# A fused state-space scan and ELU feed-forward block on one Trainium2 core: three changes of order in the opening, a weight load ahead of a B load, a negative part ahead of a weight piece's magnitude, and a clamp and shift ahead of two masks

## The chip, the core and the metric

The kernel runs on one core of a Trainium2 chip. The core has a matrix engine (TensorE, PE in the profile, with its weight loads as PEld), a vector engine (VectorE, DVE), an activation engine (ScalarE, ACT), a general engine (GpSimd, POOL), a queue engine that here only issues transfers (SyncE, SP), and 16 DMA engines. Each engine takes its own instructions strictly in the order in which they were written. Engines wait for one another by semaphores. The metric is the time of one execution on the device in microseconds. Lower is better.

## The reference

The first half is a chunked state-space scan ("mamba2_ssd") over 4 batches, 8 heads and 768 tokens, with 32 channels per head and a state of 16. The second half is a feed-forward block with an ELU between its two matrix products, on 3072 tokens of width 256 and a hidden width of 2048.

```python
cum = np.cumsum(la, axis=-1)                         # la = log of clipped a, per chunk
L = np.exp(cum[:, :, :, None] - cum[:, :, None, :])  # times the causal mask
M = np.einsum('bhin,bhjn->bhij', Cc, Bc) * L
y = np.einsum('bhij,bhjd->bhid', M, xc) + np.einsum('bhin,bhnd->bhid', Cc, state) * np.exp(cum)[..., None]
state = decay_full * state + np.sum(Bx, axis=2)      # Bx = B x, each step decayed to the chunk's end
...
h = x @ w_in                                         # x is y with heads and channels side by side
g = np.where(h > 0.0, h, np.exp(np.minimum(h, 0.0)) - 1.0)
return (g @ w_out).astype(np.float32)
```

The two weight matrices are handed over as 64-bit floats. [...]

## The kernel before

The tokens are worked in twelve blocks of 256, numbered 0 to 11: block 0 and block 1 are the first 256 tokens of two batches, 2 and 3 the next 256 of the same two, and so on. For each block the scan makes a 256 x 256 slab `yT`, and the feed-forward part multiplies it by pieces of `w_in` (`l1`), applies the ELU (`elu`), and multiplies by pieces of `w_out` (`l2`). The order of all instructions is written out by hand: there is no scheduler that moves them, and the statements at the end of the kernel function are that order.

There are 16 weight pieces, 0 to 7 of `w_in` and 8 to 15 of `w_out`, each 512 KB as 64-bit words. A piece is turned into 32-bit floats by these steps, and the names come back in all that follows:

- `w_load` (line 184) issues the transfer on SP.
- `w_abs` (205, ACT) takes the magnitude of the high words. For pieces 1 and 2 it writes to PSUM, the matrix engine's accumulator memory; for the others to SBUF, the main on-chip memory.
- `w_low` (214, ACT) brings the low words into a small float.
- `w_sign` (229, DVE) takes the sign bit, SBUF to SBUF.
- `w_high_a` (237, DVE) clamps the magnitude. It runs in PSUM for piece 2 and from SBUF to SBUF for piece 3.
- `w_high_b` (244, DVE) shifts the magnitude and joins the sign. `w_high` is `w_high_a` and then `w_high_b`.
- `w_sum` (254, POOL) adds the low part. After it the piece can be used by `l1`.

The ELU of one product is three instructions. `begin_elu` (731, ACT) takes the negative part with a Relu of the negated product. `elu` then issues the Exp (738, ACT) and the join (739, DVE). `elu` calls `begin_elu` itself unless it has been called already.

Block 1's part of the scan in the opening needs: B and C in the "square" and the token layout. `load_bc(1)` loads B for the two halves of the tokens as two transfers of 64-byte rows (140); `load_squares(1, 1)` loads C (124). `turn_square(1, 1)` (468, DVE) transposes C in 32 x 32 blocks. `turn_b(1)` transposes B on PE (432) and copies it on ACT (435). `mask_heads(1)` multiplies the turned C by two head masks, two DVE instructions (478), which write `ctm`. `turn_exp(1)` (459, DVE) multiplies the turned C by the decay `ec`; both its inputs lie in SBUF. `scores(1)` (583, PE) needs `ctm` and the turned B. `weigh` (592, DVE) multiplies the scores by the decays `L`. `sums(1)` (613, PE) and `states(1)` (628 and 630 on DVE, 635 on POOL) make the running states. `across(1)` (661, PE) and `inside(1)` (679, PE) make block 1's result, which ACT and DVE copy to `yT` (696, 694). On POOL, `scaled(1)` (423) multiplies B by a decay, and `rest_of_sums` (343) prepares decays for the later blocks; it stands right behind `w_sum(3)`.

After that the long middle begins with `l1(1, 0)`, the first product on block 1's result.

The part of the written order that the change touches reads, before:

```python
w_abs(2); w_low(2, nc.scalar); w_high_a(2); w_sign(2); w_high_b(2); w_sum(2)
elu()
turn_square(1, 1)
first_decays(1, 0, 1, 2, 3); l1(0, 1); w_abs(3)
w_low(3, nc.scalar); w_sign(3)
mask_heads(1)
w_high(3)
turn_b(1)
```

Of the kernel before, what the change touches and what calls it, by code (L numbers as in the profile page):

```python
# [33 lines left out]
def kernel(  # L34
# [56 lines left out]
    def psum(shape, name):  # L91
        return p_a.tile(shape, F32, tag="a", name=name)
# [18 lines left out]
    def place(n):  # L111

        return 2 * (n // (2 * NG)) + n % 2, n // 2 % NG
# [5 lines left out]
    def load_squares(n, k):  # L119
        b, g = place(n)  # L120
        squares = st[n]["bc"].rearrange("p k u h n -> p k (u h n)").rearrange(
            "p k (m r) -> p k m r", m=2)
        for m in range(2):
            nc.sync.dma_start(
                out=squares[:, k, m],
                in_=(B, C)[k][b, m:NH:2, g * BLK:(g + 1) * BLK, :].rearrange(
                    "q (c t) n -> q c (t n)", t=8))

    def load_bc(n, c_queue=nc.sync, us=(0, 1)):
        b, g = place(n)  # L130
        if "bc" not in st.setdefault(n, {}):
            st[n]["bc"] = raw.tile([P, 2, 2, NH, N], F32, tag="bc", name="bc", bufs=2)
        if n > 3:
            for k in range(2):
                load_squares(n, k)
            return
        for u in us:
            sl = slice((2 * g + u) * P, (2 * g + u + 1) * P)
            for k, src in enumerate((B,) if n == 1 else (B, C)):
                (nc.sync, c_queue)[k].dma_start(  # L140
                    out=st[n]["bc"][:, k, u], in_=src[b, :, sl, :].rearrange("h s n -> s h n"))
# [50 lines left out]
    def w_words(i):  # L192
        words = w_raw[i].rearrange("p k (f t) -> p k f t", t=2)
        return words[:, :, :, 0], words[:, :, :, 1]

    def w_parts_of(i):
        if i not in w_mag:
            both = big([P, 2, 2, CW], U32, "mag")
            w_mag[i], w_sgn[i] = both[:, 0], both[:, 1]

    def w_abs(i, cols=slice(None)):
        if i in (1, 2) or cols.start:
            w_abs_of[i, cols.start] = psum([P, 2, CW], "ps_mag").bitcast(U32)
        w_parts_of(i)
        nc.scalar.activation(
            w_abs_of.get((i, cols.start), w_mag[i])[:, :, cols].bitcast(F32),
            w_words(i)[1][:, :, cols].bitcast(F32), ACT.Abs)
# [4 lines left out]
    def w_low(i, eng, cols=slice(None)):  # L212
        if eng is nc.scalar:
            eng.activation(  # L214
                pieces[i][0][:, :, cols], w_words(i)[0][:, :, cols], ACT.Identity,
                scale=2.0 ** -51, bias=two)
        else:
            eng.tensor_scalar(
                out=pieces[i][0], in0=w_words(i)[0], scalar1=2.0 ** -51, scalar2=2.0,
                op0=ALU.mult, op1=ALU.add)  # L220

    def w_sign(i, cols=slice(None), eng=nc.vector):
        w_parts_of(i)
        if eng is nc.gpsimd:
            eng.tensor_scalar(
                out=w_sgn[i][:, :, cols], in0=w_words(i)[1][:, :, cols].bitcast(mybir.dt.int32),
                scalar1=0.0, scalar2=2.0 ** 31, op0=ALU.is_lt, op1=ALU.mult)
            return
        nc.vector.tensor_scalar(
            out=w_sgn[i][:, :, cols], in0=w_words(i)[1][:, :, cols], scalar1=0x80000000,  # L230
            scalar2=None, op0=ALU.bitwise_and)

    def w_high_a(i, cols=slice(None)):
        mag = w_abs_of.get((i, cols.start), w_mag[i])[:, :, cols]


        nc.vector.tensor_scalar(
            out=mag.bitcast(F32), in0=mag.bitcast(F32),
            scalar1=high_word_as_f32(0x38000000), scalar2=high_word_as_f32(0x47EFFFFF),
            op0=ALU.max, op1=ALU.min)  # L240

    def w_high_b(i, cols=slice(None), ks=slice(None)):
        mag, sgn = w_mag[i][:, ks, cols], w_sgn[i][:, ks, cols]
        nc.vector.scalar_tensor_tensor(
            out=mag, in0=w_abs_of.get((i, cols.start), w_mag[i])[:, ks, cols], scalar=3, in1=sgn,
            op0=ALU.logical_shift_left, op1=ALU.bitwise_xor)

    def w_high(i):
        w_high_a(i)
        w_high_b(i)  # L250

    def w_sum(i, cols=slice(None), ks=slice(None)):
        w = pieces[i][0].bitcast(U32)[:, ks, cols]
        nc.gpsimd.tensor_tensor(out=w, in0=w_mag[i][:, ks, cols], in1=w, op=ALU.add)  # L254
# [172 lines left out]
    def turn_b(n):  # L427

        s = st[n]
        tb = psum([P, 2, P], "ps_tb")  # L430
        for u in range(2):
            nc.tensor.transpose(
                out=tb[:, u], in_=s["bc"][:, 0, u].rearrange("p h n -> p (h n)"),
                identity=ident)
        nc.scalar.copy(out=s["bt"], in_=tb)
# [25 lines left out]
    def turn_square(n, k):  # L461


        s = st[n]
        if "squares" not in s:
            s["squares"] = att.tile([P, 2, 2, P], F32, tag="bct", name="bct", bufs=2)
            s["bt"], s["ct"] = s["squares"][:, 0], s["squares"][:, 1]
        nc.vector.transpose(
            out=s["squares"][:, k].rearrange("p u i -> p (u i)").rearrange("p (c t) -> p t c", t=8),
            in_=s["bc"].rearrange("p k u h n -> p k (u h n)").rearrange(  # L470
                "p k (m t n) -> p k t m n", m=2, n=N)[:, k])

    def mask_heads(n, eng=nc.vector):
        s = st[n]
        s["ctm"] = att.tile([P, 2, 2, P], F32, tag="ctm", name="ctm")
        if eng is nc.vector:
            for k in range(2):
                eng.tensor_scalar(
                    out=s["ctm"][:, :, k], in0=s["ct"], scalar1=hmask2[:, k:k + 1],
                    scalar2=None, op0=ALU.mult)  # L480
            return
        eng.tensor_tensor(
            out=s["ctm"], in0=s["ct"].unsqueeze(2).to_broadcast([P, 2, 2, P]),
            in1=hmask2.unsqueeze(1).unsqueeze(3).to_broadcast([P, 2, 2, P]), op=ALU.mult)
# [22 lines left out]
    def first_cum(n):  # L507

        for k in range(2):
            for v in range(2):  # L510
                for q in range(4):
                    rows, row = slice(32 * q, 32 * q + 32), 32 * q + NH * n + 2 * q + k
                    nc.tensor.matmul(
                        out=st[n]["low"][q][Q * v:Q * v + Q, k],
                        lhsT=ident[rows, row:row + 1].to_broadcast([32, Q]),
                        rhs=F0[rows, :, Q * v:Q * v + Q], start=False, stop=False,
                        tile_position=(32 * q, Q * v), skip_group_check=True)
        for u in range(2):
            for q in range(4):
                rows, r0 = slice(32 * q, 32 * q + 32), 32 * q + NH * n + 2 * q  # L520
                nc.tensor.matmul(
                    out=st[n]["low"][q][:, :, u], lhsT=F0[rows, u],
                    rhs=minus[rows, r0:r0 + 2].unsqueeze(2).to_broadcast([32, 2, Q]),
                    start=False, stop=True, tile_position=(32 * q, 0), skip_group_check=True)
# [179 lines left out]
    def g_tile(n, i):  # L704

        if (n // 2, i) not in g_of:
            g_of[n // 2, i] = big([P, 2, 2, BLK], F32, "g")
        return g_of[n // 2, i]
# [19 lines left out]
    def begin_elu():  # L728

        begun.append(ffn.tile([P, 2, BLK], F32, tag="e", name="e", bufs=2))  # L730
        nc.scalar.activation(begun[0], lag[0][2], ACT.Relu, scale=-1.0)

    def elu():
        if not begun:
            begin_elu()
        n, i, ps = lag.pop(0)
        e = begun.pop()
        nc.scalar.activation(e, e, ACT.Exp, scale=-1.0)
        nc.vector.scalar_tensor_tensor(
            out=g_tile(n, i)[:, :, n % 2], in0=e, scalar=1.0, in1=ps,  # L740
            op0=ALU.subtract, op1=ALU.max)
# [303 lines left out]
    w_load(1)  # L1045
    load_bc(1, us=())
    load_squares(1, 1)
    load_bc(1, us=(0,))
    w_load(2)
    load_bc(1, us=(1,))  # L1050
    w_load(3)
    load_x(1, 4)
    half = [slice(0, P), slice(P, 2 * P)]
# [47 lines left out]
    spread_cum(2)  # L1101
    first_low(1, p_o)
    first_cum(1)
    w_abs(2)
    w_low(2, nc.scalar)
    w_high_a(2)
    w_sign(2)
    w_high_b(2)
    w_sum(2)
    elu()  # L1110
    turn_square(1, 1)
    first_decays(1, 0, 1, 2, 3)
    l1(0, 1)
    w_abs(3)
    w_low(3, nc.scalar)
    w_sign(3)
    mask_heads(1)
    w_high(3)
    turn_b(1)
    nc.scalar.activation(F[:, 1], F[:, 0], ACT.Exp)  # L1120
    write_flat_exp()
    load_bc(2)
# [356 lines left out]
```

## Time and profile before

| what | value |
| --- | --- |
| median of 3 runs | 341.44 us (341.13 to 341.68) |
| the profiled execution's own time | 342.17 us |
| its span from first to last instruction | 340.5 us, 9647 instructions |
| PE busy | 333.4 us, 98% of the span |
| DVE, ACT, POOL busy | 286.5, 259.2, 214.9 us |
| granted TensorE clock | 1.00 throughout |

PE is busy nearly all the time. Cut into stretches of the span, PE is busy for 308.70 us of the 312.15 us from 28.35 us to the end, and for 24.7 us of the 28.35 us before that. So an order that makes PE wait longer or shorter in the opening moves the whole of the rest, and the opening is the place to read.

In the profile's groups a line of this kernel can stand for many uses. Line 254 is the last step of every weight piece, and line 739 the join of every early ELU. The reader has to go by time within the opening to tell them apart. Start times below are from the span's start.

### The profile page before, as it was taken

To read this page: it belongs to the slowest core of one execution; us is meant where nothing else is said; L and a number is where in the kernel's file an instruction comes from. 1 tells how busy PE (TensorE), PEld (TensorE's weight loads), DVE (VectorE), ACT (ScalarE), POOL (GpSimd) and SP (SyncE) were. 2 spreads that over 40 slices of the span, in tenths; PEclk is the share of its full clock that TensorE was granted. 3 is DMA by queue.
4 is the path that set the end of the run, shared out by engine and by line. 5 is a ranking of instruction groups with operands and counts; after the bars stand their busy time and mean duration, and the time that the engine had idled before them with its cause. 6 is when DMAs were issued, how large, how long until landed. Compare 5 with 4: busy or idle time off the path is not lost.

```text
span 340.5 us, 9647 instructions
## 1 busy us (share of the span) xinstructions
PE 333.4 (98%) x3742; PEld 289.8 (85%) x3742; DVE 286.5 (84%) x509; ACT 259.2 (76%) x537; POOL 214.9 (63%) x242
## 2 busy tenths in 40 slices
PE   8889999999999999999999999999999999999996
PEld 6568878888888888888899888899888899999995
DVE  3798988889897889898989998989995977997951
ACT  4598989699858599857898866898866789897501
POOL 5644545456979396988578978478984346685000
PEclk9999999999999999999999999999999999999999
DMA  8899999372578378570869591769441754230101
GB/s 136 207 249 169 315 184 267 80 148 73 190 145 316 119 184 301 176 204 14 277 184 184 179 276 26 272 181 172 135 166 29 253 166 142 93 128 0 34 0 62
DMA packets 82955, 54.79 MB, mean 161 GB/s; under 512 B 59038, under 2 KB 68574, under 8 KB 82910
## 3 DMA queue, kind: packets, MB, share of 16 engines
q1 hardware_dynamic: 80734, 53.98, 56.7%
q8 instruction: 29, 0.48, 0.6%
q10 hardware_dynamic: 2176, 0.20, 0.5%
q14 instruction: 16, 0.13, 0.1%
HBM read 44.53 MB, written 9.63 MB: 159 GB/s over the span
## 4 chain that ended last, share of the span: by engine, by line
PE 91%; SPq 3%; ACT 2%; DMA 2%; DVE 1%; issue 0%; POOL 0%; DVEq 0%; ACTq 0%
PE ps_o L982 24%; PE ps_h L833 20%; PE ps_o L886 12%; PE ps_h L718 10%; PE ps_w L833 10%; PE ps_both L982 6%; PE ps_y L679 3%; PE ps_y L661 2%; DMA w<-in_moe_w_in_dram 2%; PE ps_g L583 2%; PE ps_st L613 1%; PE ps_high L982 1%; SPq L184 1%; SPq L140 0%; SPq L156 0%; ACT w_in L214 0%
## 5 line engine op out<-in xcount | busy, mean ns | idle before, releaser
L900 POOL TENSOR_TENSOR g_words<-g_words,g_low 128x512 fp32r<-128x512 f32 x62 | 82.5, 1333 | 51.1 <-DVE g_low L924 28.4
L982 PE MATMUL ps_o<-o_words,g_words 128*128 128x256 f32 x448 | 83.7, 284 | 0.0
L982 PEld LDWEIGHTS ps_o<-o_words,g_words 128*128 128x128 f32 x448 | 72.7, 191 | 6.1 <-POOL g_words L900 1.1
L861 ACT ACTIVATE e<-ps_h 128x512 f32<-128x512 f32 x72 | 43.1, 598 | 36.3 <-DVE ps_h L849 36.3
L868 DVE SCALAR_TENSOR_TENSOR g<-e,ps_h 128x512 f32<-128x512 f32 x72 | 49.2, 684 | 19.3 <-ACT e L862 17.0
L924 DVE SCALAR_TENSOR_TENSOR g_low<-g_words,g 128x512 fp32r<-128x512 f32 x72 | 63.8, 891 | 0.0
L982 PE MATMUL ps_o<-o_low,g_low 128*128 128x256 f32 x224 | 63.3, 283 | 0.0
L849 DVE SCALAR_TENSOR_TENSOR ps_h<-ps_h,e 128x512 f32<-128x512 f32 x72 | 49.7, 691 | 2.7 <-ACT e L841 2.6
L833 PE MATMUL ps_w<-y_both,w_words 128*128 128x512 f32 x144 | 48.7, 419 | 0.0
L718 PE MATMUL ps_h<-yT,w_in 128*128 128x256 f32 (+1 forms) x208 | 45.2, 367 | 2.4 <-POOL w_in L254 2.4
L841 ACT ACTIVATE e<-ps_w 128x512 f32<-128x512 f32 x72 | 42.0, 583 | 7.3 <-PE ps_w L833 7.3
L862 ACT ACTIVATE e<-e 128x512 f32<-128x512 f32 x72 | 45.5, 632 | 2.3
L886 PE MATMUL ps_o<-w_out,g 128*128 128x256 f32 x192 | 45.5, 380 | 0.0
L833 PE MATMUL ps_h<-y,w_words 128*128 128x512 f32 x144 | 45.4, 396 | 0.1
L833 PE MATMUL ps_h<-y,w 128*128 128x512 f32 x144 | 44.6, 391 | 0.0
L923 ACT ACTIVATE g_words<-g 128x512 fp32r<-128x512 f32 x72 | 43.6, 625 | 0.0
L718 PEld LDWEIGHTS ps_h<-yT,w_in 128*128 128x128 f32 x208 | 36.3, 190 | 8.4 <-POOL w_in L254 3.5
L982 PEld LDWEIGHTS ps_o<-o_low,g_low 128*128 128x128 f32 x224 | 42.7, 191 | 0.0
L886 PEld LDWEIGHTS ps_o<-w_out,g 128*128 128x128 f32 x192 | 36.1, 189 | 5.4
L833 PEld LDWEIGHTS ps_h<-y,w_words 128*128 128x128 f32 x144 | 26.6, 188 | 7.0 <-PE ps_w L833 0.9
L833 PEld LDWEIGHTS ps_h<-y,w 128*128 128x128 f32 x144 | 27.0, 188 | 6.2
L833 PEld LDWEIGHTS ps_w<-y_both,w_words 128*128 128x128 f32 x144 | 23.6, 191 | 1.9 <-DVE y_both L817 0.2
(133 smaller groups left out, 552.3 us busy)
## 6 DMA issues: line engine op xcount, KB each, us to landing
w_words<-w_kept SPq DMA_DIRECT2D x28, 512.0 KB
w<-w_kept SPq DMA_DIRECT2D x28, 256.0 KB
L<-flat SPq DMA_DIRECT2D x20, 256.0 KB
w<-in_moe_w_out_dram SPq DMA_DIRECT2D x8, 512.0 KB
w_kept<-w_words SPq DMA_DIRECT2D x8, 512.0 KB
w<-in_moe_w_in_dram SPq DMA_DIRECT2D x7, 512.0 KB
xr<-in_x_dram SPq DMA_DIRECT2D x24, 128.0 KB
out_dram<-eo SPq DMA_DIRECT2D x18, 128.0 KB
```

The source lines that it names most:

```text
L718: nc.tensor.matmul(out=ps[:, j, toks], lhsT=w_in[i][:, k, j * P:(j + 1) * P], rhs=yT[n // 2][:, k, n % 2].rearrange("p u i -> p (u i)")[:, ...
L833: nc.tensor.matmul(out=ps, lhsT=lhs[:, k], rhs=rhs[:, k], start=k == 0 and lhs is not w0, stop=k == KC - 1 and lhs is not w1)
L841: nc.scalar.activation(e, both, ACT.Copy, scale=WORD)
L849: nc.vector.scalar_tensor_tensor(out=high, in0=high, scalar=WORD - 1.0, in1=e, op0=ALU.mult, op1=ALU.add)
L861: nc.scalar.activation(e, high, ACT.Relu, scale=-1.0)
L862: nc.scalar.activation(e, e, ACT.Exp, scale=-1.0)
L868: nc.vector.scalar_tensor_tensor(out=g_tile(n, m // 2)[:, m % 2].rearrange("p b i -> p (b i)"), in0=e, scalar=1.0, in1=h, op0=ALU.subtract ...
L886: nc.tensor.matmul(out=o_of[n][:, ts], lhsT=g_of[n // 2, j][:, m % 2, n % 2, ts * P:(ts + 1) * P], rhs=w_out[j][:, m % 2], start=(m == 0 a ...
L900: nc.gpsimd.tensor_tensor(out=out, in0=in0, in1=in1, op=ALU.subtract)
L923: yield nc.scalar.activation(words[:, 0], g, ACT.Copy, scale=NEAR / WORD)
L924: yield nc.vector.scalar_tensor_tensor(out=low, in0=words[:, 0].bitcast(F32), scalar=WORD, in1=g, op0=ALU.mult, op1=ALU.subtract)
L982: nc.tensor.matmul(out=ps, lhsT=lhs, rhs=rhs, start=lhs is both_g and first > 0 or lhs is g1 and first > 1, stop=last and lhs is not g1, s ...
```

## The change

Three things are put in another order. No instruction is added or removed.

1. On SP, the load of weight piece 2 goes ahead of the first half of block 1's B. The two halves of B then follow one another.
2. `begin_elu` for the first product goes ahead of piece 2's magnitude on ACT, so that only its Exp is left behind piece 2's low words. On DVE, the transposition of C goes ahead of the first ELU's join.
3. On DVE, piece 3's clamp and shift (`w_high(3)`) go ahead of the two masks of C. On ACT, the copy of the turned B goes ahead of piece 3's low words.

```diff
     w_load(1)
     load_bc(1, us=())
     load_squares(1, 1)
-    load_bc(1, us=(0,))
     w_load(2)
-    load_bc(1, us=(1,))
+    load_bc(1)
     w_load(3)
     load_x(1, 4)
...
     spread_cum(2)
     first_low(1, p_o)
     first_cum(1)
+    begin_elu()
     w_abs(2)
     w_low(2, nc.scalar)
     w_high_a(2)
     w_sign(2)
     w_high_b(2)
     w_sum(2)
+    turn_square(1, 1)
     elu()
-    turn_square(1, 1)
     first_decays(1, 0, 1, 2, 3)
     l1(0, 1)
     w_abs(3)
+    turn_b(1)
     w_low(3, nc.scalar)
     w_sign(3)
+    w_high(3)
     mask_heads(1)
-    w_high(3)
-    turn_b(1)
     nc.scalar.activation(F[:, 1], F[:, 0], ACT.Exp)
```

The order on PE and on POOL is the same before and after.

## The prediction

> **What bounds the kernel now.** I read the page's busy shares and its chain first, then the chain in order of time for the opening, then the order of DVE and POOL there, and last the places where a DVE and a POOL instruction meet.
>
> ```profile
> PE 333.4 (98%) x3742; PEld 289.8 (85%) x3742; DVE 286.5 (84%) x509; ACT 259.2 (76%) x537; POOL 214.9 (63%) x242
> ...
> PE 91%; SPq 3%; ACT 2%; DMA 2%; DVE 1%; issue 0%; POOL 0%; DVEq 0%; ACTq 0%
> ```
>
> ```profile
> 28.35:340.50 312.15, 308.70 (x3232) 272.22 (x3232) 266.71 (x458) 240.70 (x493) 200.17 (x206) 1.00 0.55 158
> ```
>
> From 28.35 us on PE works without a stop that matters (busy 308.70 of 312.15 us in the stretch of the second fence). The kernel's time moves with the start of the first product on block 1, at 28.35. This is the chain that leads there:
>
> ```profile
> 9.98 6.41 DMA w<-in_moe_w_in_dram
> ...
> 16.47 0.63 ACT ps_mag L205
> ...
> 19.89 0.69 ACT mag L205
> ...
> 23.27 0.69 DVE g L739
> ...
> 25.21 0.14 DVE S_new L628
> ...
> 28.35 1.67 PE ps_h L718 x11
> ```
>
> Weight piece 2 lands at 16.39; its magnitude starts at 16.47 on ACT, after 2.11 us of idling. ACT then carries the chain until the second ELU's join on DVE at 23.27. From there DVE runs back to back to the states at 25.13, and PE follows. What the join's 23.27 becomes is what 28.35 becomes. Now the two engines that the third edit touches:
>
> ```profile
> 20.05 0.54 DVE L229 TENSOR_SCALAR mag<-w 128x512 uint32<-128x512 uint32 x1
> 20.51 0.97 DVE L478 TENSOR_SCALAR ctm<-bct,hmask 128x256 f32<-128x256 f32 x2
> 21.40 0.42 DVE L237 TENSOR_SCALAR mag<-mag 128x512 f32<-128x512 f32 x1
> 21.85 0.69 DVE L244 SCALAR_TENSOR_TENSOR mag<-mag 128x512 uint32<-128x512 uint32 x1
> 22.46 0.42 DVE L459 TENSOR_TENSOR bct<-bct,ec 128x256 f32<-128x256 f32 x1
> ```
>
> ```profile
> 19.02 1.28 POOL L254 TENSOR_TENSOR w_in<-mag,w_in 128x512 uint32<-128x512 uint32 x1 [2.45 <-ACT e L738]
> 20.26 0.81 POOL L423 TENSOR_TENSOR sc<-bc,eb 128x256 f32<-128x256 f32 x1
> 22.69 1.33 POOL L254 TENSOR_TENSOR w_in<-mag,w_in 128x512 uint32<-128x512 uint32 x1 [1.62 <-ACT e L731]
> 23.98 0.60 POOL L343 TENSOR_TENSOR la<-F 96x256 f32<-96x256 f32 x1
> ```
>
> The sign of piece 3 (20.05) takes 0.54 us where the same form takes 0.41 (17.74): it ends 0.29 after POOL's sum at 20.30. The first mask then takes 0.71 and ends 0.15 after POOL's `scaled` (21.07); the second, beside nothing, takes 0.34. POOL's sum of piece 3 starts only behind the shift (22.54), when the masks are long done. A later stage shows the meeting at full length:
>
> ```profile
> 70.27 1.27 POOL L254 TENSOR_TENSOR w_out<-mag,w_out 128x512 uint32<-128x512 uint32 x1 [1.09 <-DVE mag L244]
> 70.71 1.12 DVE L218 TENSOR_SCALAR w_out<-w 128x512 f32<-128x512 uint32 x1
> ...
> 71.75 0.42 DVE L229 TENSOR_SCALAR mag<-w 128x512 uint32<-128x512 uint32 x1
> ```
>
> A DVE instruction from SBUF to SBUF, 0.42 alone (54.27), takes 1.12 because it ends 0.29 after POOL's sum. So a `TENSOR_SCALAR` of DVE between SBUF and SBUF stands until the POOL instruction under way is over. DVE instructions with two SBUF inputs do the same: the low part of g at 189.55 (line 924) takes 1.32 instead of 0.68 and ends 0.55 after a POOL sum that ended at 190.32. The Trainium skill, SBUF — State Buffer, section Who interferes with whom, states the rule: DVE in its two-port mode, or with two SBUF inputs against a GpSimd instruction that reads SBUF, shares a port pair with GpSimd, and whichever issues first holds it for its whole instruction. By that rule the third edit costs time, and the rows above agree; by lengths alone, without it, the sum below would come to 0.73 us less than now instead of 0.65 more.
>
> **The change part by part.** Nothing is added, so each part is a matter of who stands behind whom.
>
> *Piece 2 ahead of B.* On SP, the issue that takes 2.35 us (9.98) moves past one B issue (0.47, at 9.47); the issues behind the pair keep their place. That stall belongs, I estimate, to the many rows queued ahead of it, since piece 3's issue took 0.58; then it falls to B now. Half of B is 1024 rows of 64 bytes, 64 per DMA engine, at about 10.5 ns a row in the transfer records: up to 0.67 us on the engine that finishes last, of which I take 0.5. Piece 2 then lands near 15.9. Bounds: no earlier at all (16.39), or, if the stall vanishes, some 2 us earlier. The Trainium skill, DMA: Bandwidth & Descriptors, section Queues, rings and completion order, says that each DMA engine takes descriptors in ring order; no run here has yet shown this swap. By it piece 2 gains what B's rows take; without it the third rival's time holds. B's second half keeps its place in the queue; it landed at 17.76 in the completion records, and PE's transposition wants it at 18.83: hidden, with 1.07 us of slack. The two x transfers, wanted by `sums(1)` at 22.91, landed by 21.56.
>
> *Relu ahead of the magnitude.* The first product's last matmul ends at 15.35 (14.97 plus 0.38); a Relu follows its product by about 0.04 (65.12 behind 65.08) and takes 0.60, and ACT's next starts about 0.05 before its end. So the magnitude of piece 2 can start at 15.95 at the earliest, which caps the gain of the first part. I take T = 16.0 for it, against 16.47. Behind it ACT has 0.6 us less: low words, Exp, four decays (from about 17.75), then piece 3's magnitude at 19.14, since piece 3 landed at 19.06. It was 19.89. Everything of ACT comes about 0.7 us earlier; the copy of B costs the low words of piece 3 another 0.26 and they still end at 20.8, before POOL asks for them. The transposition and the first join only swap places on DVE: nothing waits for either in between, cost nothing; the cover is gone only if `ctm` were wanted before 19.6.
>
> *Clamp and shift ahead of the masks.* From T, by the steps of before (clamp +0.66, sign +0.61, shift +0.45, its end +0.69):
> - shift of piece 2 ends at 18.41; POOL's sum starts 0.14 later (as 19.02 behind 18.88), 18.55 to 19.83.
> - piece 3's sign, ready at 19.5, waits: ends 0.29 later, 20.12. `scaled` takes 0.62 alone (7.71) and resumes behind the sign: ends 20.60, as before 0.48 behind the sign.
> - the clamp, now next, waits for `scaled`: 20.60 + 0.29 = 20.89. Shift: +0.03 +0.69 = 21.61. It was 22.54, so 0.93 us have been won up to here.
> - POOL's sum of piece 3 starts at 21.75 (+0.14). The first mask runs 21.53 to 21.87 (0.34). The second can ask for the ports only when the first is through, by when the sum has asked: from the rows above a DVE mask asks about 0.19 after its recorded start, at 21.98, and POOL about 0.14 after its own, at 21.89. The sum goes first, for 1.33 (its length before; 1.28 alone): to 23.08. The second mask ends 0.15 later, 23.23.
> - `rest_of_sums`, behind the sum on POOL, has waited since then and goes next: it is through at 23.70 (0.60, less the 0.14 ahead of its asking). `turn_exp` has two SBUF inputs and stands behind it: +0.29 = 23.99.
> - the second ELU's join, next on DVE, starts 0.08 before that, at 23.91. It was 23.27: 0.65 us later (rounded).
>
> Scores start at about 23.3 instead of 22.28, in time for `weigh`, which comes 0.6 behind the join. Behind the join DVE runs back to back as before, so the states, `across` and the product at 28.35 come 0.65 later, and PE has no later idle time to take it up. The later transfers land well ahead (the nearest, piece 6, at 32.63 for a use at 34.51).
>
> Sum: 0.93 won up to the shift's end; from there to the join it was 0.73 (22.54 to 23.27, part of it a wait for the Exp) and becomes 2.30 (21.61 to 23.91), 1.57 lost: +0.65 after rounding. The profiled execution of 342.17, with its span of 340.5, would go to 342.8 and 341.15; the median of the runs shown is 0.73 below that execution, so the forecast for it is 341.44 + 0.65 = 342.1.
>
> **The rivals.**
> - *The ports do not hold the masks (faster).* Then DVE goes on from the shift at 21.61 and ACT sets the end: magnitude of piece 3 at 19.14 instead of 19.89, Exp of the second ELU done at 22.5, join at 22.54, 0.73 us earlier: 340.7. It decides if the second mask ends before 22.0 and `turn_exp` is not held. For it: the clamp and ACT do come earlier. Against: every row that I read of a DVE two-port instruction beside a POOL one was held. Chance 0.10.
> - *The second mask gets the ports first.* The race is 0.09 us by my reading of two offsets. Then the sum runs 22.0 to 23.28, `turn_exp` is held to 23.57 and the join starts at 23.49: +0.22, 341.7. Chance 0.15.
> - *Piece 2 lands no earlier* because the long issue stays with it: T = 16.47, everything 0.47 later: +1.1, 342.55. For it: the 2.35 us have no releaser in the profile. Against: the 64-byte rows queued ahead. Chance 0.15.
> - *B comes late for PE.* With both halves together the second one would have to slip by over 1.07 us to hold PE's transposition, and by over 2 for scores at 23.3; some 343 then. Chance 0.05.
>
> **How the numbers follow.** The main case has 0.55 and runs from +0.55 (T = 15.95, a sum of 1.28) to +0.85. A change of 0.2%, 0.68 us, is about what a measurement of this kernel can tell from none; the main case straddles it, and I put 0.32 of its 0.55 above, since each further wait and wake-up only adds. Slower: 0.32 + 0.15 + 0.05 = 0.52. Faster: most of the first rival, 0.08. The same: the rest, 0.40. The range from 341.3 to 342.7 leaves out the first and the last rival and holds the others with the spread of the runs; the likeliest case's own is 341.9 to 342.4.
>
> **What would show it.** In the changed profile: piece 2's magnitude near 16.0 with a Relu ahead of it; piece 3's shift ending near 21.6; one mask of about 0.34 and one of about 1.4 us, or a pair of 1.7; POOL's sum of piece 3 from about 21.75; the join of the second ELU near 23.9 and the product on block 1 near 29.0. Two masks of 0.34 each would show the lock wrong, a sum that starts only behind both would show the race wrong, and a magnitude at 16.47 the first part. A first product on block 1 before 28.3 would make the forecast wrong in sign.

## The result and the profile after

The changed kernel takes 343.12 us (median; 342.45 to 344.26), the kernel before 341.30 us on the same chip. The ratio is 1.0061, 95% interval 1.0046 to 1.0077: slower by 1.8 us by the medians and by 2.1 us by the ratio, which is not formed from the medians; 0.65 was forecast. The profiled execution took 342.77 us with a span of 341.1.

The page's busy shares, its chain, and the stretch from the first product on block 1 to the end:

```profile
PE 333.0 (98%) x3742; PEld 289.7 (85%) x3742; DVE 287.7 (84%) x509; ACT 259.1 (76%) x537; POOL 215.3 (63%) x242
...
PE 86%; DVE 4%; ACT 3%; POOL 2%; SPq 1%; issue 1%; DMA 1%; DVEq 0%; POOLq 0%
```

```profile
28.52:341.10 312.58, 308.69 (x3234) 272.37 (x3232) 266.74 (x458) 240.75 (x493) 200.32 (x206) 1.00 0.55 158
```

PE works as long as before from that product on (308.69 us busy against 308.70). The stretch itself is some 0.4 us longer. About half of that is one more wait, right behind the product's first two matmuls, until 29.11 (the last row of the next fence). So the opening is still the place to read. The shares of the chain (PE 86% instead of 91%) do not tell that: the chain runs through other waits in the long middle, without PE's work there being longer. The chain in order of time leads to `l1(1, 0)` like this now:

```profile
13.95 1.15 PE ps_h L718 x4
15.14 0.47 issue
15.61 0.64 ACT ps_mag L205
...
23.45 0.67 DVE g L739
...
29.11 0.49 PE ps_h L718 x2
```

Before, the chain came to piece 2's magnitude from its transfer. Now it comes from PE's first product; the piece called issue is the time in which ACT ran the Relu. This is the opening on ACT, and then on DVE and POOL (start, length, engine, line, operation, tiles):

```profile
15.12 0.60 ACT L731 ACTIVATE e<-ps_h 128x512 f32<-128x512 f32 x1 [1.16 <-PE ps_h L718]
15.61 0.64 ACT L205 ACTIVATE ps_mag<-w 128x512 f32<-128x512 f32 x1
```

```profile
20.53 0.69 DVE L244 SCALAR_TENSOR_TENSOR mag<-mag 128x512 uint32<-128x512 uint32 x1
21.14 1.64 DVE L478 TENSOR_SCALAR ctm<-bct,hmask 128x256 f32<-128x256 f32 x2
22.88 0.65 DVE L459 TENSOR_TENSOR bct<-bct,ec 128x256 f32<-128x256 f32 x1
23.45 0.67 DVE L739 SCALAR_TENSOR_TENSOR g<-e,ps_h 128x512 f32<-128x512 f32 x1
```

```profile
21.36 1.27 POOL L254 TENSOR_TENSOR w_in<-mag,w_in 128x512 uint32<-128x512 uint32 x1 [1.15 <-DVE mag L244]
22.58 0.66 POOL L343 TENSOR_TENSOR la<-F 96x256 f32<-96x256 f32 x1
```

The two masks, which took 0.97 us together before, take 1.64: singly 0.346 and 1.378, and the second ends at 22.776, 0.15 after POOL's sum of piece 3 (22.63). `turn_exp`, 0.42 before, takes 0.65, behind POOL's `rest_of_sums`. These are the two holds that the forecast described. The magnitude of piece 2 starts at 15.61, directly behind the Relu, which waited for PE.

From here on T is the start of piece 2's magnitude, and the stretch is the time from T to the second ELU's join.

| | T | stretch | join | first product on block 1 | block 2's first transposition (L443) |
| --- | --- | --- | --- | --- | --- |
| before, first trace | 16.47 | 6.80 | 23.27 | 28.35 | 39.11 |
| forecast for it | 16.0 | 7.91 | 23.91 | 29.0 | |
| after | 15.61 | 7.84 | 23.45 | 28.52 | 39.47 |

The stretch is right within 0.07 us. But at the last column these two executions differ by 0.36 us only, and the medians differ by 1.8. So one of the two traces is not an ordinary one, or something comes on top that this one does not show.

### The profile page after: what moved, and what is told of

It reads as the page before. It is cut to its first block, busy times and chain, and to the rows that moved or that the text cites. A ratio compares the mean times of both kernels' runs of the same rounds, so it can differ in the third digit from the quotient of the medians.

```text
span 341.1 us, 9648 instructions
## 1 busy us (share of the span) xinstructions
PE 333.0 (98%) x3742; PEld 289.7 (85%) x3742; DVE 287.7 (84%) x509; ACT 259.1 (76%) x537; POOL 215.3 (63%) x242
## 4 chain that ended last, share of the span: by engine, by line
PE 86%; DVE 4%; ACT 3%; POOL 2%; SPq 1%; issue 1%; DMA 1%; DVEq 0%; POOLq 0%
PE ps_o L982 24%; PE ps_h L833 20%; PE ps_w L833 10%; PE ps_o L886 10%; PE ps_h L718 8%; PE ps_both L982 6%; PE ps_y L679 3%; PE ps_y L661 2%; PE ps_g L583 2%; DMA w<-in_moe_w_in_dram 1%; PE ps_high L982 1%; DVE g L739 1%; PE ps_st L613 1%; POOL w_out L254 1%; DVE mag L244 1%
```

## The experiments

All ratios are to the kernel before on the same chip, with 95% intervals. The theory: the lock between DVE and POOL (a DVE instruction stands until POOL's is over) costs what was forecast, and the start T, taken from one late execution, is what was mis-sized. The first rival: the masks are long for a reason other than POOL's sum. The second: the load's new place makes the opening late.

**The kernel before and the changed kernel again.** No edit.

> The kernel before, unchanged, for a second trace. Late-base theory: the trace that the forecast was worked on (342.17 us) lies 0.87 us above the median of six runs (341.3) because its opening was late, so an ordinary execution has piece 2's magnitude on ACT well before 16.47 us and the second ELU's join 0.4 to 0.9 us before 23.27. Rival, later stage: the opening is always as in the first trace (magnitude at 16.47 +- 0.15, join at 23.27 +- 0.15), and what differs between executions lies behind 28 us. Ratio to the kernel before: 1.000 +- 0.001 by both.

> The changed kernel, unchanged, for a second trace and a second set of times. Lock theory: one mask of about 0.35 us and one of about 1.4, turn_exp held to the end of rest_of_sums, the join near 23.5, however early piece 2 lands, since the Relu caps its start near 15.6 to 16.0. Late-base theory: ratio to the kernel before again near 1.006, though this trace alone differs from the first one of before by only 0.6 us. Later-stage rival: a stall of PE over 0.5 us somewhere behind 30 us that before does not have.

Measured: before again 341.58 us, ratio 0.999 (0.9975 to 1.0005), the changed kernel 343.36, ratio 1.0051 (1.0031 to 1.0070). The kernel before has this row now, on ACT:

```profile
15.62 0.64 ACT L205 ACTIVATE ps_mag<-w 128x512 f32<-128x512 f32 x1 [1.40 <-DMA w<-in_moe_w_in_dram]
```

Piece 2 landed at 15.53 instead of 16.39, T is 15.62, and the stretch is 6.78. In the changed kernel T is 16.12, 1.66 behind the start of the first product's second half, and the stretch 7.86. So the stretches repeat, to 0.02 us, and T does not. Nor is a later stage the cause: from block 2's first transposition to the end it takes 300.95 to 301.43 us in the four profiled executions of the kernel before and 301.17 to 301.60 in the four of the changed one.

**The third part alone, and the first two parts without it.** On the kernel before, only

```diff
     w_abs(3)
+    turn_b(1)
     w_low(3, nc.scalar)
     w_sign(3)
+    w_high(3)
     mask_heads(1)
-    w_high(3)
-    turn_b(1)
```

and then everything but this.

> Only clamp and shift ahead of the masks, and the copy of B ahead of piece 3's low words; loads and Relu as before. Lock theory: second mask about 1.4 us, turn_exp behind rest_of_sums, join 1.1 us later than before: ratio 1.003, and over 1.004 if an ordinary execution of before has an earlier opening than its first trace. If the lock were not the cause: ratio 1.000, masks of 0.35 to 0.7 us.

> The changed kernel with the masks ahead of clamp and shift again, as before, and the copy of B behind the low words; so only the load's and the Relu's new places are left. Lock theory: both masks done before POOL's sum of piece 3, join at 22.3 to 22.6, faster than before by up to 0.7 us on the first trace's base: ratio 0.998. Late-base theory: less of that gain, ratio 0.9985 to 1.000, as before has it in an ordinary execution. If the load or the Relu were what makes the changed kernel slow: ratio 1.003 to 1.006.

Measured: the third part alone 342.83 us, ratio 1.0035 (1.0018 to 1.0053), stretch 7.86, masks of 0.346 and 1.384 us. Without the third part 341.57, ratio 0.9986 (0.9972 to 0.9999), stretch 6.34. DVE without the third part:

```profile
20.64 0.97 DVE L478 TENSOR_SCALAR ctm<-bct,hmask 128x256 f32<-128x256 f32 x2
...
22.59 0.42 DVE L459 TENSOR_TENSOR bct<-bct,ec 128x256 f32<-128x256 f32 x1
22.93 0.68 DVE L739 SCALAR_TENSOR_TENSOR g<-e,ps_h 128x512 f32<-128x512 f32 x1
```

The third part alone lengthens the stretch by 1.06 us (7.86 from 6.80), and beside the other two by 1.50 (7.84 from 6.34). The loss belongs to it, and the second part in fact shortens the stretch by 0.44 (6.36 with it alone, below). But the join of this execution came at 22.93, not at 22.3 to 22.6, since its T was 16.59; that is later than in ordinary executions of the kernel before (22.40 to 22.51), so the trace does not show where the 0.9986 comes from.

**The masks between the clamp and the shift.** In the changed kernel `w_high_a(3)`, then the masks, then `w_high_b(3)`, so that POOL's sum cannot be asked for before the masks are through.

```diff
-    w_high(3)
+    w_high_a(3)
     mask_heads(1)
+    w_high_b(3)
```

> The changed kernel with one thing altered: the two masks stand behind piece 3's clamp and ahead of its shift, so the sum on POOL cannot be asked for before the masks are through; the clamp still goes ahead of the masks. Lock theory: both masks take 0.34 to 0.41 us unless `scaled` is under way, the sum starts behind the shift near 22.5, `turn_exp` is held at most by the start of that sum, and from the start of piece 2's magnitude to the second ELU's join it takes 6.3 to 6.7 us instead of 7.84; the ratio to the kernel before is 0.998 to 1.000. Rival (the earlier clamp, or the copy of B ahead of the low words, is what costs): the stretch stays at 7.5 or more and the ratio near 1.005.

Measured: 341.21 us, ratio 1.0002 (0.9988 to 1.0016). On DVE:

```profile
21.26 0.60 DVE L478 TENSOR_SCALAR ctm<-bct,hmask 128x256 f32<-128x256 f32 x2
21.78 0.68 DVE L244 SCALAR_TENSOR_TENSOR mag<-mag 128x512 uint32<-128x512 uint32 x1
22.39 0.41 DVE L459 TENSOR_TENSOR bct<-bct,ec 128x256 f32<-128x256 f32 x1
22.72 0.67 DVE L739 SCALAR_TENSOR_TENSOR g<-e,ps_h 128x512 f32<-128x512 f32 x1
```

The pair of masks takes 0.60, `turn_exp` 0.41, and the stretch is 6.31. The early clamp and the early copy of B cost the stretch nothing. T was 16.41 in this execution, behind the Relu, which takes back what the shorter stretch gains.

**The sum held back until the masks are through.** The order of DVE stays as changed; POOL gets one more instruction ahead of piece 3's sum, a copy of one column of `ctm` that nobody reads.

```diff
     scaled(1, nc.gpsimd)
+    nc.gpsimd.tensor_copy(held_back, st[1]["ctm"][:, 1, 1, P - 1:P])
     w_sum(3)
```

> The changed kernel in its own order on DVE, ACT, PE and SP, with one tiny copy added on POOL (one column of the masked C, into a tile that nobody reads) ahead of piece 3's sum, so that the sum waits until the second mask is through. This makes POOL wait longer and adds an instruction. Lock theory: two masks of about 0.34 us, the second one no longer held; the sum starts behind them, near 22.2, and can then hold `turn_exp`, which asks at about the same time: if it does, the join comes at most 0.3 us earlier than in the changed kernel and the ratio stays near 1.004; if `turn_exp` gets in first, the stretch from piece 2's magnitude to the join falls to 6.3 to 6.6 us and the ratio to 0.998 to 1.000. Rival (the masks are long for a reason other than the sum): the second mask stays at 1.4 us and the time rises by the added wait, ratio 1.005 to 1.008.

Measured: 342.41 us, ratio 1.0039 (1.0022 to 1.0056). On DVE (the lines are one higher here, since the copy's tile is declared ahead of them):

```profile
22.57 0.61 DVE L479 TENSOR_SCALAR ctm<-bct,hmask 128x256 f32<-128x256 f32 x2
23.29 0.42 DVE L460 TENSOR_TENSOR bct<-bct,ec 128x256 f32<-128x256 f32 x1
23.63 0.68 DVE L740 SCALAR_TENSOR_TENSOR g<-e,ps_h 128x512 f32<-128x512 f32 x1
```

The same DVE order with a later sum gives masks of 0.61 for the pair and a stretch of 6.60. Making POOL wait longer shortened the opening's stretch by 1.24 us. That leaves the sum as the cause of the long mask, and the first rival falls. The ratio, expected at 0.998 to 1.000 for such a stretch, stayed above. In the profiled execution the first product's second half started late, at 15.37, and T with it (17.03): ACT had waited 1.90 us for the first half of weight piece 0, which landed at 11.60, where it landed at 9.30 to 10.57 in the other fifteen. Whether that holds for this version's other executions is open.

**The first part alone, and the second part alone**, each on the kernel before.

```diff
-    load_bc(1, us=(0,))
     w_load(2)
-    load_bc(1, us=(1,))
+    load_bc(1)
```

```diff
+    begin_elu()
     w_abs(2)
...
-    elu()
     turn_square(1, 1)
+    elu()
```

> The kernel before with the first part alone: the load of piece 2 ahead of the first half of B. If the load was what piece 2's magnitude waited for, the magnitude starts 0.5 to 0.9 us earlier than in an ordinary execution of the kernel before (15.6), and some of that reaches the join: ratio 0.998 to 0.9995. If the load alone gains nothing, because piece 3's landing or the order on ACT and DVE sets the join, the ratio is 1.000 plus or minus 0.001. If the long issue stays with piece 2, the magnitude stays at 15.6 or later.

> The kernel before with the second part alone: the Relu ahead of piece 2's magnitude on ACT and the transposition of C ahead of the first join. Piece 2 then lands as before, near 15.5, and the Relu fits into ACT's wait for it, so the magnitude starts near 15.7 and the chain behind it is 0.4 to 0.6 us shorter on ACT: stretch from magnitude to join 6.3 instead of 6.78, ratio 0.998 to 0.9995. Rival (piece 3's landing bounds the chain, so the room on ACT gains nothing): stretch 6.7 to 6.8 and ratio 1.000.

Measured: the load alone 340.79 us, ratio 0.9986 (0.9975 to 0.9998), T 15.17, stretch 6.80. The Relu and the transposition alone 341.43, ratio 1.0005 (0.9994 to 1.0016), T 15.73, stretch 6.36. On ACT, with the load alone and then with the Relu and the transposition alone:

```profile
15.17 0.64 ACT L205 ACTIVATE ps_mag<-w 128x512 f32<-128x512 f32 x1 [0.45 <-DMA w<-in_moe_w_in_dram]
```

```profile
15.23 0.60 ACT L731 ACTIVATE e<-ps_h 128x512 f32<-128x512 f32 x1 [1.16 <-PE ps_h L718]
15.73 0.64 ACT L205 ACTIVATE ps_mag<-w 128x512 f32<-128x512 f32 x1
```

The load alone lets the magnitude follow the earlier landing (15.09); 15.17 is 0.45 earlier than an ordinary 15.62, just under what was expected. With the Relu ahead of it, the magnitude follows the first product instead. Piece 2 had landed at 15.35 there, and the magnitude stood behind the Relu until 15.73. The second part shortens the stretch by 0.44, as expected, and the time not at all, where 0.998 to 0.9995 was expected.

**The kernel before twice more, and the changed kernel once more.**

> The kernel before once more, to see where piece 2's magnitude ordinarily starts. If the first trace (16.47, landing 16.39) was a late one, it starts at 15.5 to 15.8, as in the second trace (15.62) and in the third part alone (15.71). If 16.47 is ordinary, it is at 16.2 to 16.6. Stretch to the join 6.78 to 6.80.

> As the run beside it: the kernel before once more, piece 2's magnitude at 15.5 to 15.8 if the first trace was a late one, 16.2 to 16.6 if it was ordinary; stretch to the join 6.78 to 6.80.

> The changed kernel once more. Piece 2 lands early and its magnitude starts behind the Relu, 1.66 us after the second half of the first product starts on PE: between 15.6 and 16.6, by where that half starts (13.95 to 14.93 so far). If the load moved ahead paid, it would be under 15.5. Stretch to the join 7.84 to 7.86.

Measured: before 340.99 and 341.38 us, T 15.71 and 15.56, stretches 6.80 and 6.90. Changed 343.04 us, T 16.26, stretch 7.85. Of four profiled executions of the kernel before, three have T between 15.56 and 15.71; the first, at 16.47, was 0.8 us late.

**A pause of PE.** In the changed kernel block 1's `inside` takes longer than 0.88 us. PE in the changed kernel run again, where this is largest:

```profile
27.67 0.44 PE L679 MATMUL ps_y<-M,xr 64*32 64x64 f32 x28
28.32 0.62 PE L679 MATMUL ps_y<-M,xr 64*32 64x64 f32 x36 [0.21 <-issue]
```

PE stops behind the 28th matmul without waiting for anything that the profile shows. The pause stood behind the 28th in all five executions that have it: the changed kernel three times, the third part alone, and the masks between clamp and shift. It delays the copies of the result, so that `l1(1, 0)` waits once more: from the join to block 2's first transposition it takes 15.96 to 16.26 us in these five and 15.84 to 15.86 in all the others except one (below). The trace's transfers of kind instruction, 16 KB each, suggest why: the third of them ended at 25.64 to 27.10 in these five, and each time PE went on 1.2 to 1.5 us later. In the executions without a pause that had been profiled by then it ended by 25.06. (In the fourth of the changed kernel, below, it ended at 27.01 without a pause, but there PE came to this place only at 29.5.) To test it, 14 of the first 58 tiny warm-up matmuls were left out, which produce nothing that is read.

```diff
-    small_idle_products(29)
+    small_idle_products(22)
```

> The changed kernel with 14 fewer of the tiny warm-up matmuls at its start (7 of 29 calls, two matmuls each), whose result nobody reads. It asks what PE's pause inside block 1's `inside` is, which stood right behind its 28th matmul in four executions. If PE waits there for the next block of its own instructions (the trace has such blocks of 16 KB, and the one in question ended at 25.6 to 27.1 us in just these four executions and by 25.1 in the six without a pause), the pause moves by 14 matmuls, to behind the 42nd, or is gone if the block comes early. If it is a wait for data (the decayed scores or x), it stays behind the 28th. The rest of the opening stays: stretch from piece 2's magnitude to the second ELU's join 7.8 to 7.9, ratio to the kernel before 1.004 to 1.006.

Measured: 343.63 us, ratio 1.0084 (1.0058 to 1.0109), above what was expected; the stretch is 7.85. Block 1's `inside` has no pause, but block 0's has one:

```profile
11.15 0.45 PE L679 MATMUL ps_y<-M,xr 64*32 64x64 f32 x30
12.83 0.53 PE L679 MATMUL ps_y<-M,xr 64*32 64x64 f32 x34 [1.23 <-issue]
```

The first instruction transfer ended at 11.24 here, where it ends at 7.5 to 9.1 in the other executions, and PE went on 1.59 us behind it. That is the same sequence at another place, and this execution's third transfer ended at 27.40, more than 2 us ahead of the 42nd matmul of block 1's `inside` (about 29.6). The place fits too. Of PE's matmuls, weight loads and semaphore instructions in the trace, 962 stand ahead of the pause in all five executions, and 449 ahead of block 0's pause here. That is 513 apart, and the third transfer is two blocks, 32 KB, behind the first: 64 bytes an instruction. All 29 transfers of this queue bring 0.48 MB for 7588 such instructions in the changed kernel, 63 bytes each. So the pauses stand where one block of instructions ends and are, by all this, waits for the next; the run did not show the pause behind the 42nd, since the block had come by then. When such a transfer is asked for, the trace does not tell, and why the third one is late under the changed order stays open.

**The Relu left late.** The changed kernel without `begin_elu()` ahead of `w_abs(2)`, beside the changed kernel itself.

```diff
-    begin_elu()
     w_abs(2)
```

> The changed kernel with the Relu of the first product back behind piece 2's low words on ACT; all else as changed. If the early Relu is what keeps piece 2's magnitude from the earlier landing, the magnitude starts by the landing, at 15.1 to 15.3 as with the load alone (15.17), instead of 15.6 to 16.3; ACT then carries the Relu behind it, and the stretch to the second ELU's join is 7.8 to 8.1 (the third part's cost stays). Join near 23.1, time 0.5 to 0.9 us under the changed kernel's: ratio to the kernel before 1.002 to 1.004. Rival (the opening of the changed kernel is late for another reason, the load's place on the queue among them): magnitude at 15.6 or later, ratio 1.005 to 1.006.

> The changed kernel again, for the comparison with the run beside it on the same chip: ratio 1.005 to 1.006, magnitude of piece 2 at 1.66 us behind the second half of the first product, 15.6 to 16.6, stretch 7.84 to 7.86, and from the join to block 2's first transposition 15.96 to 16.23 instead of 15.84.

Measured: with the Relu late 342.14 us, ratio 1.0022 (1.0012 to 1.0033); the changed kernel 343.11, ratio 1.0050 (1.0032 to 1.0068). With the Relu late the magnitude waits for its data again:

```profile
15.43 0.64 ACT L205 ACTIVATE ps_mag<-w 128x512 f32<-128x512 f32 x1 [0.49 <-DMA w<-in_moe_w_in_dram]
```

Piece 2 landed at 15.35, and the first product's second half only started at 14.82, so that behind the Relu the magnitude would have started at 16.48 (1.66 later). T, 15.43, is 0.13 over what was expected, the stretch, 8.19, 0.1 over, and the join comes at 23.62 instead of 23.1, but the ratio is inside the expected bounds, and the time 0.97 us under the changed kernel's. So the second of the rivals of this section falls as well: with the load in its new place the magnitude starts a little earlier than ordinarily (15.43 against 15.56 to 15.71), once the Relu does not stand in front.

The profiled execution of the changed kernel beside it took 344.35 us, and shows one thing more. PE, and the granted clock by stretches (the eighth column, ahead of the DMA share):

```profile
24.04 0.70 PE L583 MATMUL ps_g<-ctm,bct 32*64 32x128 f32 x32 [1.43 <-ACT e L738]
24.67 0.49 PE L613 MATMUL ps_st<-xr,sc 64*32 64x64 f32 x32
25.39 3.54 PE L718 MATMUL ps_h<-yT,w_in 128*128 128x256 f32 x8 [0.23 <-DVE g L739]
```

```profile
22.20:25.60 3.40, 1.74 (x67) 1.06 (x67) 3.30 (x7) 2.93 (x6) 1.88 (x2) 1.00 0.78 196
25.60:29.01 3.41, 3.41 (x16) 2.23 (x23) 3.21 (x10) 0.44 (x1) 1.17 (x4) 0.50 0.83 92
29.01:31.00 1.99, 1.98 (x94) 1.62 (x94) 0.82 (x3) 1.12 (x4) 0.00 (x0) 0.99 1.07 298
```

The profile puts the scores' wait of 1.43 us down to an Exp of ACT; it was the second mask, which ended at 23.90, 0.14 ahead of the scores. Behind a stretch in which PE was busy for 1.74 of 3.40 us, its clock was granted at 0.50 for 3.41 us, and the eight matmuls of the third product took 3.54 us instead of 1.97. From the join to block 2's first transposition it took 16.90 us instead of 15.84. The same wait of 1.43 us stands in the other three profiled executions of the changed kernel, which kept the full clock. The times of the changed kernel are of two groups: 15 of 22 executions lie between 342.45 and 343.42 us, 7 between 344.00 and 344.35, none in between. The one profile from the upper group has the half clock, the three from the lower one have not. The clock granted on average over an execution says the same: it is 0.995 in all seven, as 3.41 us at half clock in 341 make it, and 0.998 to 1.000 in the other fifteen and in every execution of the kernel before.

## Why the prediction was right or wrong

**The third part: right in its mechanism and its size.** Measured from T, the forecast's steps came out as follows. Shift of piece 3 ended: 5.61 forecast (21.61 less 16.0), 5.61 measured (21.22 less 15.61). Sum of piece 3 on POOL: 5.75 and 5.75. Masks: 0.34 and then held until 0.15 behind the sum; measured 0.346 and 1.378. Join: 7.91 and 7.84. First product on block 1: 13.0 and 12.91. The prediction's first rival, that the ports do not hold the masks, is dead, and so is its second, where the second mask goes first: the sum went first in all five profiled executions with this order of sum and masks (the changed kernel four times, the third part alone) and in the two variants of it with fewer warm-up matmuls and with the late Relu. Its fourth, that B comes late, falls too: PE had no idle time ahead of the transposition of B in any of the four. The rule that the forecast drew from the Trainium skill, SBUF — State Buffer, section Who interferes with whom, that the shared port is held for a whole instruction, agrees with the 1.378 us of the second mask.

**The first part: right about the transfer, wrong about what the sum was taken from.** Moved ahead of B, piece 2's issue takes 0.47 us and the long stall falls to B (2.68 for its two), as estimated, and to piece 3 (2.72 instead of 0.58), which the estimate left out; piece 3 landed no later for it (17.46 in the first trace after, 19.06 in the first before). Piece 2 lands at 14.30 to 15.69, mean 14.96, in ten profiled executions with the load moved, and at 15.35 to 16.39, mean 15.67, in six without: some 0.7 us earlier, where 0.5 was taken. The prediction's third rival, that it lands no earlier, falls. Alone, the move is worth 0.4 to 0.5 us (T 15.17, ratio 0.9986).

**The step that failed is "I take T = 16.0 for it, against 16.47".** Two things were wrong with this pair.
- The 16.47 was a late execution's. The profiled execution lay 0.73 above the median, and the forecast subtracted that at the end as if it were spread evenly. It sat in the very wait that the first part was to shorten. Ordinary executions have 15.56 to 15.71.
- The Relu's cap was named in the forecast (15.95), but as a bound on a gain. Against an ordinary T it is a loss. In the four profiled executions of the changed kernel T was 15.61, 16.12, 16.26 and 16.67, mean 16.17, each time 1.66 behind the start of the first product's second half (13.95 to 15.01). That start was settled ahead of the change: it comes 5.34 to 5.47 us behind block 0's `turn_exp`, which starts at 8.48 to 9.66, when the moved load has only just been issued (8.50 to 10.07) or not yet. Why block 0 is at times later is open.

So instead of -0.47 the term is +0.54 (16.17 less 15.63, the mean of the three ordinary ones). With the +1.06 that the stretch measured, where the forecast had 7.91 less 6.80, that is +1.6 already.

**"PE has no later idle time to take it up" was true, but the way from the join to the middle was taken as fixed.** It is 0.13 to 0.39 us longer by the instruction wait in three of the changed kernel's four profiled executions, and 1.06 by the half clock in the fourth: on average 0.44. The sum is +0.54 + 1.06 + 0.44 = 2.0 us. Measured were 1.0061, 1.0051 and 1.0050 times 341.3, that is 1.7 to 2.1. The sum rests on four profiled executions, in which T and the clock differ from one to the next, so the agreement to a tenth is in part luck.

The forecast's "nothing waits in between, cost nothing" for the swap of transposition and first join held: with the second part alone the stretch even fell, by 0.44, since the Relu was done ahead of the magnitude. That gain, and the load's, are the only ones in the change. The first is lost beside the third part, which costs 1.50 there instead of 1.06, and the early Relu gives back the second.

The best of the versions run are the load alone and the first two parts without the third, both at 0.9986, some 0.5 us under the kernel before. The load alone is the one whose gain is understood.

## What to carry to other kernels

Before a wait of a profiled execution is credited as a gain, ask where that execution differs from the median: a surplus of the size of the expected gain may sit in that very wait, and a second trace of the unchanged kernel settles it. A Relu, or any instruction, that is put ahead of a transfer's consumer on an in-order engine should depend on nothing that can be later than the transfer. And work that shortens one engine's chain can bring another engine's long instruction beside short ones that it then holds; a version with a deliberate wait on that engine tells this apart.

## What the runs showed of the hardware that was not expected

- PE waits for its own instructions, as far as the places and times show. Six profiled executions show a pause of 0.15 to 1.2 us inside a row of small matmuls, 1.2 to 1.6 us behind the end of a 16 KB instruction transfer.
- The clock can fall to half without a long gap. The Trainium skill, TensorE: Matmul & The Clock Gate, Part 1, has the clock go down after an idle window of about 3.4 us. Here it went down behind a stretch that was busy for 1.74 of 3.40 us and whose longest wait was 1.43. The length at half clock, 3.41 us, agrees with the Trainium skill. A second case is the kernel with fewer warm-up matmuls, where PE's clock was 0.50 from 13.98 to 17.40 us, behind the 1.23 us instruction wait. In all sixteen traces the clock records change only in steps of 3.413 us; from the first clock record on, the full clock lasted five such steps in the one and two in the other, and the half clock one step in both. The step ahead of the half clock had PE busy for 1.75 us in the one and 2.00 in the other. In the three profiled executions of the changed kernel that kept the full clock the least busy step had 1.98 or 1.99. So how a wait falls on the steps matters, but the profile's busy time alone does not tell where the limit lies.
- One instruction more on POOL, a copy of one column that made the sum wait, took 1.24 us out of the stretch that it stood beside.
